# Seven products in place of eight in the input layer of two batches of a routed attention and Silu feed-forward kernel

## The chip, the cores and the metric

The kernel runs on one core of a Trainium2 chip. Its engines work side by side, each through its own list of instructions in order: TensorE (PE in the profile, with its weight loads as PEld), VectorE (DVE), ScalarE (ACT), GpSimd (POOL) and SyncE (SP), which here only issues transfers. The metric is the device time of one execution in microseconds.

## The reference

Four batches of eight heads attend over 768 tokens of 64 numbers each. Queries and keys are assigned to the nearest of 16 centroids of their head, and a query sees only keys of its own cluster. The heads' outputs are put side by side (512 numbers a token, 3072 tokens) and go through a feed-forward layer with 2048 hidden features:

```python
q_assign = np.argmax(np.einsum('bhsd,hcd->bhsc', q_n, c_n), axis=-1)
k_assign = np.argmax(np.einsum('bhsd,hcd->bhsc', k_n, c_n), axis=-1)
mask = q_assign[:, :, :, None] == k_assign[:, :, None, :]
scores = np.where(mask, scale * np.matmul(q, k.transpose(0, 1, 3, 2)), -1000000000.0)
attn = np.exp(scores - max); attn = attn / (attn.sum + 1e-09)
x = (attn @ v) laid out as (B * S, H * D)
h = x @ w_in                          # 512 -> 2048
g = h * (1.0 / (1.0 + np.exp(-h)))    # Silu
out = g @ w_out                       # 2048 -> 512
```

## The kernel before, in words

**Attention.** Queries and keys are split into a high and a low 16-bit part (`hi`, `lo`, lines 97 to 114), transposed by DMA (`ht`, line 121) into tiles of the pool "ab" (12 tiles), compared with the centroids (`l`, line 159; `ls`, `mx`, `ge` on VectorE), and the one-hot result is transposed and copied into the same tiles (`cs`, `cx`, `cv`), so that one product gives scores that are far apart where the clusters differ. A unit of attention (`qk`, line 333, and `ex`, line 338) is a pair of score products over one half of the queries (384 tokens) and one Exp over 128x768 into a tile of the pool "P" (13 tiles). Six units make two heads, which `pv` (line 350) weights with the values in 36 matmuls; `nm` divides, and `xd` (a DMA transpose on SP, line 389) or `pt` and `pe` (a transpose on TensorE and a copy) put the result, transposed, into `xts[b, c]`: batch b, half c of the tokens, four chunks of 128 numbers.

**Input layer.** For each batch, half c and block fb of 128 hidden features, `e` runs four matmuls over the four chunks (line 398) into a PSUM bank, `t` takes Tanh of half the sum into a float tile of the pool "tn" (3 tiles, line 410), and `g` (line 413, VectorE) multiplies (Tanh + 1) with the sum, which is twice the Silu, into `gt`. That is 32 units a batch, 128 in all.

**Output layer.** Pairs of token tiles (`Pair`, the `duos`) are multiplied by seven products in place of eight: `S` are sums on VectorE (line 498), `m` the products of eight matmuls (line 485), `z` copies a bank out on ScalarE (line 507), `o` combines and sends the result (lines 513 to 522), with a factor 0.5 that takes back the doubled Silu. The engine letters behind `z` and `o` in the plan have no effect.

**The order** of everything is a plan written out by hand as one list of words. A word is an operation and its number, with a letter for the engine and digits for the PSUM bank where it needs one. `step` turns each word into instructions, so each engine's order is the order of the words that concern it. Four PSUM banks are numbered 0 to 3; the other four form two double banks (tag "st") for the scores. Exp and Tanh are both read from one activation table, which is loaded once (line 567). SP's queue holds the loads, the DMA transposes and the stores in plan order; POOL's holds some loads, `cv` and casts.

Of the kernel before, what the change touches and what calls it, by code (L numbers as in the profile page):

```python
# [29 lines left out]
def kernel(  # L30
# [289 lines left out]
    NU = len(units)  # L320
    pst, Ps = {}, {}

    def qk_mm(u):
# [4 lines left out]
        qj, qn = qc[i, c]

        rhs = abs_[qj.name][:, qn : qn + 3, :].rearrange("p n c -> p (n c)")  # L330
        for e in range(2):
# [1 line left out]
            nc.tensor.matmul(pS[:, e, 0:HALF], abs_[kj.name][:, kn, :], rhs, start=True, stop=True)  # L333
# [119 lines left out]
    class Pair:  # L453

        def __init__(self, b, x, y):
            self.b, self.x, self.y = b, x, y
# [47 lines left out]

        def snap(self, n):
            o = self.half(*((0, 0), (1, 0), (1, 1))[n])
            nc.scalar.activation(out=o, in_=self.xb[:, 0:DH], func=AF.Copy, bias=0.0, scale=0.5)  # L507

        def out(self, r, c):
            t = (self.x, self.y)[r]  # L510
            o = self.half(r, c)
            if (r, c) == (0, 1):
                nc.scalar.activation(out=o, in_=self.xb[:, 0:DH], func=AF.Copy, bias=0.0, scale=0.5)
            else:
                i = self.yb[:, 0:DH] if r == 0 else self.wb[:, DH:DM]
                nc.vector.scalar_tensor_tensor(out=o, in0=i, scalar=0.5, in1=o, op0=ALU.mult, op1=ALU.add)  # L516
# [95 lines left out]
    def step(op, n, eng, banks):  # L612
# [149 lines left out]
        o11.D o10 qk86 lo24 ex86 lo22 t34 g34 qk90 ex90 pv13.1 e42.3 nm13 qk88 t42 g42 ex88 xd12 e35.0 t35 l20.2 qk93
        ex93 cx19 ge18 cs18 ht22 g35 e41.1 t41 v16.P qk91 ex91 e37.3 t37 ls20 mx20 ge20 hi23.D e39.0 qk89 t39 ex89
        qk85 g37 ex85 cx18 g39 g41 e45.2 l21.3 ls21 qk92 t45 r26 g45 e44.0 t44 g44 e46.1 lo23 mx21 ex92 ge21 qk94 ex94
        cv17 pv14.3 nm14 t46 qk100 ex100 qk95 ex95 v26.A g46 cs20 e33.2 t33 cx20 e47.0 t47 qk99 ex99 g47 pv15.3 nm15
        qk98 ex98 xd13 e43.1 t43 g33 g43 e40.0 qk97 m21.3 t40 g40 ht23 vl21.P cv20 cv19 ex97 xd14 v21.A qk101 ex101
        S23 xd15 qk109 S21 S22 l22.2 ls22 m22.1 l23.0 z20.A m26 ls23 mx23 ex109 cv18 cs21 z21.A cx21 qk108 ex108
        hi26.D qk96 r27 ex96 lo26 m25 z22.A v18.P ge23 vl25.P o20 qk107 ex107 e48.2 t48 g48 e57.0 qk110 ex110 S24
        qk106 ex106 pv16.1 nm16 t57 g57 cv21 qk103 ex103 e60.2 r25 qk104 t60 g60 e62.1 ex104 ht24 cs23 r28 qk113
        hi25.D cx23 cv23 m23 mx22 t62 g62 ex113 qk105 e53.0 ex105 ht26 lo25 qk102 ex102 l24.2 o21.A qk126 e55.1 ls24  # L770
        ge22 ex126 t53 v23.P vl27.P vl20 t55 g55 qk122 ex122 cs22 g53 cx22 r30 xd16 vl24.P pv17.2 nm17 qk111 ex111
        mx24 e49.3 t49 e52.1 qk112 xd17 ex112 t52 g49 l26.0 ls26 qk118 ex118 g52 hi27.D e63.2 t63 g63 e50.3 v20.P
        qk124 ex124 lo27 vl22 t50 cv22 qk131 ex131 e51.0 e56.1 t56 pv18.2 g50 qk117 t51 e59.3 ex117 hi28.D qk128 ex128
        g56 t59 e61.1 qk119 ex119 nm18 g51 lo28 e54.2 t54 mx26 ge26 cs26 g54 g59 qk116 ht25 ex116 r29 m27.0 qk115 S33
        o23 m31.2 ex115 t61 qk114 ex114 e58.3 qk127 xd18 hi30.P t58 ex127 g58 g61 S31 m37 qk125 ex125 qk121 S43 v27.A
        v22.P pv19.3 r31 l25.1 qk135 m24 ex121 S32 ls25 qk132 nm19 ex135 ht27 qk123 hi29.A m41.1 z30.D xd19 m36 o22
        z40.A ge24 m47 l27.3 ex132 m32.0 lo29 ht29 hi31.A cs24 z31.D o30 m35 cx24 S34 ex123 mx25 cv24 ls27 z32.A o33
        ht28 qk130 e72.0 ex130 t72 g72 qk120 ex120 e76.3 t76 mx27 lo30 qk142 m33 pv20.0 ge25 cs25 cx25 cx26 g76 ge27
        cs27 ex142 m34 o31.D o32 cx27 qk129 ex129 e73.3 v25.P qk134 S41 S42 vl30.P t73 nm20 g73 ex134 S44 pv21.2 ht30
        nm21 qk133 ex133 qk137 ex137 lo31 m46 z41.D qk139 e67.0 ex139 l29.3 ls29 qk140 qk136 t67 m45 g67 ex140 xd21  # L780
        qk143 cv26 z42.D l28.2 ex136 o43 e66.3 t66 ht31 g66 xd20 m43 pv22.0 nm22 ls28 cv25 vl28 mx28 cv27 xd22 ex143
        qk138 ex138 e69.3 t69 m44 g69 o41.D o42 e79.0 ge28 t79 qk141 qk147 ex141 ex147 e78.2 t78 vl31 g79 pv23.3 qk144
        g78 e64.1 t64 nm23 ex144 qk146 g64 e75.0 cs28 t75 mx29 ge29 g75 e77.2 cx28 e70.3 qk148 l30.1 ex146 t70 g70 t77
        g77 ex148 m42.0 ls30 mx30 qk154 ex154 e74.3 xd23 t74 g74 cs29 e68.2 ge30 t68 qk150 ex150 g68 e71.1 o40 e65.3
        t65 g65 qk145 ex145 t71 g71 cv28 e91.2 t91 cs30 e85.0 t85 g91 g85 v28.A e84.3 t84 qk155 S53 ex155 vl29.P l31.1
        g84 S51 ls31 e92.2 qk149 ex149 t92 g92 e82.0 qk151 S52 S54 m51.3 ex151 z50.D e81.1 t81 qk152 qk158 g81 t82 g82
        m56 mx31 ex158 v24.D e94.2 t94 e80.1 g94 pv24.0 m52.2 ex152 cx29 qk157 ex157 ge31 cv29 qk156 nm24 e89.0 z51.D
        o50 t80 e90.2 t90 g90 qk169 cx30 m57 cv30 t89 g89 ex169 ex156 m55 e95.2 cs31 cx31 z52.A o53 qk161 ex161 qk153
        cv31 e88.0 t95 g80 ex153 m53 g95 qk181 ex181 t88 qk162 ex162 m54 o51.A pv25.1 o52 nm25 qk160 ex160 e83.2 t83
        g83 qk165 ex165 e86.3 v29.D t86 g86 qk159 ex159 v30.D e87.1 t87 qk166 e93.2 t93 g87 g88 S63 m61.3 qk172 pv26.1  # L790
        ex166 qk167 ex172 m67 ex167 z60.D qk163 ex163 qk164 ex164 g93 v31.P S61 S62 S64 m66 z61.A qk171 ex171 m62.0
        m71.2 z70.D qk173 ex173 S73 nm26 xd26 xd25 qk180 ex180 o60 S71 m65 z62.D S72 qk176 m76 z71.D pv27.1 nm27 ex176
        qk190 ex190 m63 qk168 ex168 qk177 m75 ex177 qk170 ex170 m77 qk179 ex179 S74 z72.A o63 pv28.0 nm28 qk174 ex174
        xd24 qk178 m73 o73 qk175 m64 ex178 xd27 qk185 ex175 qk182 ex185 ex182 m72.1 o70 o62 e96.0 t96 m74 o72 g96
        o71.A qk184 ex184 o61.D e102.1 t102 qk183 ex183 pv29.0 nm29 e109.2 xd29 e106.3 qk189 ex189 qk188 pv30.0 g102
        t109 e110.1 g109 t106 ex188 g106 nm30 qk186 xd30 ex186 e103.2 t103 e97.3 t97 g103 qk191 ex191 g97 e101.0 t101
# [42 lines left out]
```

## Time and profile before

| | |
|---|---|
| time, median of 3 runs | 298.16 us (297.97 to 299.95) |
| the profiled execution's own time | 301.25 us |
| its span | 299.1 us |
| mean granted TensorE clock | 0.997 |
| TensorE busy | 288.4 us, 3433 matmuls |
| VectorE, ScalarE, GpSimd busy | 220.8, 233.9, 67.6 us |

The span runs from the first to the last instruction of the profiled execution. A group of instructions is shown as line, engine, operation, output and inputs, sizes and count, then the busy time and the mean duration of one in nanoseconds, then the idle time of the engine just before them and what ended it. In rows in order of time the columns are start, duration and what ran. Two instructions of one engine can overlap by a little, so the distance between starts is shorter than the duration of one.

### The profile page before, as it was taken

Reading aid. Unit: us, or ns where it says so; the run is one execution under the profiler, and the core shown is the slowest. Engines: PE = TensorE matmul, PEld = TensorE weight load, DVE = VectorE, ACT = ScalarE, POOL = GpSimd, SP = SyncE. Lnnn points to the kernel's source line nnn. Section 1 sums busy time; section 2 is a strip of 40 time slices with the busy share of each in tenths; the row PEclk is TensorE's granted clock in tenths of the full one; section 3 lists DMA queues with packets and bytes.
Section 4 is the critical chain, followed back from the end, with each engine's and each line's share of the span. In section 5 each row is a group of like instructions: output and inputs, shape, how many; then the busy total and the mean of one; then the engine's idle time right before and its main releaser. Section 6 shows DMA issues by size and latency. Waiting matters only on the chain.

```text
span 299.1 us, 8578 instructions
## 1 busy us (share of the span) xinstructions
PE 288.4 (96%) x3433; PEld 212.2 (71%) x3433; DVE 220.8 (74%) x484; ACT 233.9 (78%) x408; POOL 67.6 (23%) x127
## 2 busy tenths in 40 slices
PE   7899899999999999988999999999999999999994
PEld 3767666766677887666766878776777887677684
DVE  5898749689999888967779858677737533687763
ACT  5998899964989889986999977689688877854621
POOL 2656805220201124413142223222110000000000
PEclk9999999999999999999999999999999999999998
DMA  6999998999898979969978474962001103201103
GB/s 209 298 251 249 187 191 166 215 250 224 147 299 171 204 181 208 201 151 159 225 187 212 95 164 130 121 164 82 22 10 72 39 15 127 55 2 35 37 20 125
DMA packets 75208, 44.13 MB, mean 148 GB/s; under 512 B 54288, under 2 KB 70960, under 8 KB 75168
## 3 DMA queue, kind: packets, MB, share of 16 engines
q1 hardware_dynamic: 70272, 35.75, 51.1%
q0 software_dynamic: 4608, 7.54, 13.5%
q8 instruction: 27, 0.44, 0.6%
q10 hardware_dynamic: 288, 0.30, 0.3%
q14 instruction: 13, 0.11, 0.1%
HBM read 27.30 MB, written 6.29 MB: 112 GB/s over the span
## 4 chain that ended last, share of the span: by engine, by line
PE 53%; issue 2%; DMA 2%; POOL 1%; DVE 0%; POOLq 0%
PE ph L398 17%; PE xb L485 14%; PE pS L333 10%; PE pO L350 6%; PE yb L485 3%; DMA ab<-cdt 2%; PE wb L485 1%; PE psN L159 1%; POOL ab L217 0%; POOL vn L271 0%; POOL od L204 0%; DVE ot L516 0%; POOL od L205 0%; PE px L371 0%; POOLq L217 0%
## 5 line engine op out<-in xcount | busy, mean ns | idle before, releaser
L338 ACT ACTIVATE P<-pS 128x768 f16<-128x768 f32 x192 | 152.7, 816 | 20.3 <-PE pS L333 17.4
L398 PE MATMUL ph<-xt,win_s 128*128 128x384 f16 x512 | 96.8, 326 | 0.0
L333 PE MATMUL pS<-ab 128*128 128x384 f16 x384 | 87.9, 326 | 2.6 <-DMA ab<-cdt 1.3
L413 DVE SCALAR_TENSOR_TENSOR gt<-tn,ph 128x384 f16<-128x384 f32 x128 | 68.0, 549 | 26.2 <-ACT tn L410 25.4
L410 ACT ACTIVATE tn<-ph 128x384 f32<-128x384 f32 x128 | 62.1, 500 | 13.5 <-PE ph L398 12.7
L398 PEld LDWEIGHTS <-win_s 128*128 128x128 f16 x512 | 49.3, 98 | 31.0 <-DVE L L168 0.3
L333 PEld LDWEIGHTS <-ab 128*128 128x128 f16 x384 | 33.9, 98 | 17.5 <-DMA ab<-cdt 1.9
L350 PEld LDWEIGHTS <-P 128*128 128x128 f16 x1152 | 39.7, 98 | 4.5 <-issue 1.0
L350 PE MATMUL pO<-vt,P 128*128 128x65 f16 x1152 | 41.2, 193 | 0.8 <-DVE xn L362 0.8
L485 PEld LDWEIGHTS <-gt 128*128 128x128 f16 x352 | 34.0, 98 | 6.8
L112 DVE SCALAR_TENSOR_TENSOR hl<-raw,hl 128x768 f16<-128x768 f32 (+3 forms) x35 | 31.7, 908 | 0.7 <-ACT hl L103 0.5
L485 PEld LDWEIGHTS <-s 128*128 128x128 f16 x264 | 25.7, 98 | 5.5
L507 ACT ACTIVATE ot<-xb 128x256 f32<-128x256 f32 x33 | 12.7, 386 | 13.4 <-PE xb L485 13.3
L485 PE MATMUL xb<-wout_s,gt 128*128 128x256 f16 x176 | 22.6, 273 | 0.0
L159 PEld LDWEIGHTS <-ab 128*128 128x128 f16 x544 | 19.0, 97 | 3.7 <-DVE ab L146 0.4
L485 PE MATMUL xb<-wc,s 128*128 128x256 f16 x160 | 20.6, 273 | 0.0
L279 POOL CAST vt<-vn 128x384 f16<-128x384 f32 x19 | 10.8, 578 | 43.0 <-DMA vn<-in_v_dram 43.0
L159 PE MATMUL psN<-stk,ab 128*128 128x16 f16 (+1 forms) x544 | 19.9, 184 | 0.0
L105 POOL TENSOR_SCALAR hl<-raw 128x768 f16<-128x768 f32 (+1 forms) x8 | 15.8, 1979 | 14.1 <-DMA ab<-hl 8.4
L362 DVE TENSOR_TENSOR xn<-pO,zr 128x384 f16<-128x384 f32 x32 | 17.8, 557 | 1.1
L217 POOL DMA_DIRECT2D ab<-cdt x16 | 8.7, 546 | 40.7 <-PE pS L333 24.4
L204 POOL TENSOR_SCALAR od<-od 128x96 f16<-128x96 f16 x16 | 8.7, 542 | 38.6 <-DVE od L197 38.4
(93 smaller groups left out, 263.2 us busy)
## 6 DMA issues: line engine op xcount, KB each, us to landing
raw<-in_k_dram SPq DMA_DIRECT2D x31, 192.0 KB, 3.8
raw<-in_q_dram SPq DMA_DIRECT2D x24, 192.0 KB, 3.8
out_dram<-ot SPq DMA_DIRECT2D x18, 256.0 KB, 2.9
vn<-in_v_dram SPq DMA_DIRECT2D x19, 192.0 KB, 4.8
vn<-in_v_dram POOLq DMA_DIRECT2D x13, 192.0 KB, 4.1
win_s<-in_moe_w_in_dram POOLq DMA_DIRECT2D x8, 256.0 KB, 7.1
wout_s<-in_moe_w_out_dram POOLq DMA_DIRECT2D x4, 512.0 KB, 8.4
out_dram<-ot SPq DMA_DIRECT2D x12, 128.0 KB, 1.7
```

The lines of the kernel that those rows point to most:

```text
L105: nc.gpsimd.tensor_scalar(out=o, in0=i, scalar1=QS, scalar2=None, op0=ALU.mult)
L112: nc.vector.scalar_tensor_tensor(out=hl[:, s, 1, :], in0=raws[job.name][:, s, :], scalar=QS, in1=hl[:, s, 0, :], op0=ALU.mult, op1=ALU.sub ...
L159: nc.tensor.matmul(L[:, n % 2, :, n // 2], ab[:, i, :], stk[:, job.groups[i // 3][0], x : x + w], start=(x == 0), stop=(x + w == 2 * HC),)
L333: nc.tensor.matmul(pS[:, e, 0:HALF], abs_[kj.name][:, kn, :], rhs, start=True, stop=True)
L338: nc.scalar.activation(out=P, in_=pst.pop(u)[:, :, 0:HALF], func=AF.Exp, bias=0.0, scale=ESC)
L350: nc.tensor.matmul(o[:, (2 * t + h) * VW : (2 * t + h + 1) * VW], Ps[i + h, c, j // 2][:, j % 2, ts(t, 128)], vtb[(i + h) % 13][:, j, 0:VW ...
L362: nc.vector.tensor_tensor(out=xn, in0=ov[:, :, 0:D], in1=zr.unsqueeze(2).to_broadcast([128, 2 * NM, D]), op=ALU.mult)
L398: nc.tensor.matmul(ph[:, 0:HALF], win_s[:, r, ts(fb, 128)], xts[b, c][:, r, :], start=(r == 0), stop=(r == NR - 1))
L410: nc.scalar.activation(out=tn, in_=phs[b, c, fb][:, 0:HALF], func=AF.Tanh, bias=0.0, scale=0.5)
L413: nc.vector.scalar_tensor_tensor(out=gt[:, fb, NM * c : NM * c + NM, :].rearrange("p t n -> p (t n)"), in0=tns.pop((b, c, fb)), scalar=1.0 ...
L485: nc.tensor.matmul(o, self.lhs(l, f), self.rhs(r, f), start=(f == 0 and opens), stop=(f == HB - 1), skip_group_check=True)
L507: nc.scalar.activation(out=o, in_=self.xb[:, 0:DH], func=AF.Copy, bias=0.0, scale=0.5)
```

## The change

For batches 2 and 3 the input layer goes through seven products for each two-by-two block: the inner dimension is cut in two (chunks 0 and 1, chunks 2 and 3), the tokens in their two halves, and the features in fb and fb + 8. A group g (eight a batch) covers features g and g + 8 for both halves, in 7 products of 2 matmuls. Its words are:

- `ws` (16 in all, VectorE): sums of `w_in` halves, into four tiles of the pool "ab", one of the four in place; they serve both batches.
- `T` (four a batch, VectorE): differences of token halves, three into tiles of the pool "P", one in place.
- `y`: a product, by its number 1 to 7. Products 7 and 1 open two banks; 2 and 4 add onto the first, 6, 5 and 3 onto the second. A group uses two numbered banks or one double bank of the scores.
- `u` (VectorE or ScalarE): 0 copies the first bank out to a float tile of the pool "tn", 1 copies the second bank onto the first (PSUM to PSUM), 2 writes second + tile onto the first, 3 writes second + tile into the tile.
- `s` (ScalarE): Silu, from either bank or the tile, straight into `gt`.

The order within a group is thus 7, 1, u0, u1, 2, s0, 6, u2, 4, s2, 5, u3, 3, s1, s3. Tanh and `g` are gone for these two batches, and the output factor is 1.0 there. All Silu of a batch stand in one stretch of ScalarE's list, with no Exp between them.

The plan is the same up to word 619 (of 1551, now 1623). Behind that it is written anew: the attention of the later batches comes in another order, several `v` and `hi` words have another engine, the products of batch 2 stand between the words y161 and y223, those of batch 3 between y241 and y293.

```diff
+    def double(name):
+        return ps.tile([128, 2, 512], f32, name=name, tag="st", bufs=2)
...
+    def w_half(i, j, g, n):
+        return win_s[:, 2 * j : 2 * j + 2, i * DF // 2 + n * g : i * DF // 2 + n * g + n]
+
+    def w_sum(g, k):
+        if k == 0:
+            ws[g] = mp.tile([128, 3, 2, 256], f16, name="ws", tag="ab", bufs=12)
+        s2, s3, s4 = (ws[g][:, n] for n in range(3))
+        w = lambda i, j: w_half(i, j, g, 256)
+        o, a, b_, op = (
+            (s3, w(0, 0), w(1, 0), ALU.subtract),
+            (w(1, 0), w(1, 0), w(1, 1), ALU.add),
+            (s2, w(1, 0), w(0, 0), ALU.subtract),
+            (s4, w(0, 1), s2, ALU.subtract),
+        )[k]
+        nc.vector.tensor_tensor(out=o, in0=a, in1=b_, op=op)
+
+    def x_half(b, j, h):
+        return xts[b, h][:, 2 * j : 2 * j + 2, :]
+
+    def x_sum(b, k):
+        if k != 1:
+            tx[b, k] = mp.tile([128, 2, HALF], f16, name="tx", tag="P", bufs=13)
+        o, a, b_ = (
+            lambda: (tx[b, 0], x_half(b, 1, 1), x_half(b, 0, 1)),
+            lambda: (x_half(b, 0, 1), x_half(b, 0, 1), x_half(b, 0, 0)),
+            lambda: (tx[b, 2], x_half(b, 1, 1), x_half(b, 0, 1)),
+            lambda: (tx[b, 3], x_half(b, 1, 0), tx[b, 2]),
+        )[k]()
+        nc.vector.tensor_tensor(out=o, in0=a, in1=b_, op=ALU.subtract)
+
+    def group_mm(b, g, s, bk):
+        if s == 7 and bk == 4:
+            o = double("gd")
+            ys[b, g, 7], ys[b, g, 1] = o[:, 0, :], o[:, 1, :]
+        elif s in (7, 1) and (b, g, s) not in ys:
+            ys[b, g, s] = bank("gy" if s == 7 else "gx", bk)
+        o = ys[b, g, 7 if s in (7, 2, 4) else 1]
...
+        for r in range(2):
+            nc.tensor.matmul(
+                o[:, 0:HALF], w[:, r, :], x[:, r, :], start=(s in (7, 1) and r == 0), stop=(r == 1), skip_group_check=True
+            )
+
+    def group_mix(b, g, k, eng):
+        y, x = ys[b, g, 7][:, 0:HALF], ys[b, g, 1][:, 0:HALF] if k else None
+        if k == 0:
+            sbs[b, g] = mp.tile([128, HALF], f32, name="sb", tag="tn", bufs=3)
+        sb = sbs[b, g]
+        if k < 2:
+            o, i = (y, x) if k else (sb, y)
+            if eng == "D":
+                nc.vector.tensor_copy(o, i)
+            else:
+                nc.scalar.activation(out=o, in_=i, func=AF.Copy, bias=0.0, scale=1.0)
+        else:
+            nc.vector.tensor_tensor(out=(y, sb)[k - 2], in0=x, in1=sb, op=ALU.add)
+
+    def group_silu(b, g, j):
+        i = sbs[b, g] if j == 3 else ys[b, g, 1 if j == 1 else 7][:, 0:HALF]
+        f = g + NFB // 2 * (j // 2)
+        o = gt[:, f, NM * (j % 2) : NM * (j % 2) + NM, :].rearrange("p t n -> p (t n)")
+        nc.scalar.activation(out=o, in_=i, func=AF.Silu, bias=0.0, scale=1.0)
...
+            self.half_ = 0.5 if b < 2 else 1.0
...
+        gk = n // 10 // 8, n // 10 % 8
...
+        elif op == "ws":
+            w_sum(n // 4, n % 4)
+        elif op == "T":
+            x_sum(n // 10, n % 10)
+        elif op == "y":
+            group_mm(*gk, n % 10, bk)
+        elif op == "u":
+            group_mix(*gk, n % 10, eng)
+        elif op == "s":
+            group_silu(*gk, n % 10)
```

The plan around the entry into batch 2's products and out of them, and the entry into batch 3's:

```diff
+        ge28 cv25 qk149 ex149 nm23 xd22 l30.1 m46 z41.D v29.D cv27 qk145 ls30 xd23 ws3 hi31.D ex145 mx30 qk144 xd20
+        lo31 y161.0 m45 qk155 ex144 z42.A o43 ex155 cv26 l29.1 ls29 mx29 qk147 ex147 m34 qk154 ex154 ge29 ws12 qk150
+        ex150 m44 T20 qk148 ex148 o31.D ws13 ge30 T21 y167.1 u160.A u161.A y177.4 u170.D m43 ht31 cs28 T22 y171 ws5
...
+        cv29 u233 s232 u222 y224 s233 z50.A y233 y225 m61.0 u213 v30.P s212 u223 s231 s222 y213 S53 S51 S52 y223 s213
+        s223 m52.2 s211 qk156 s221 m56 ex156 qk153 ex153 z51.D pv24.3 cv31 qk151 ex151 qk181 ex181 m57 qk152 S54 m55
...
+        qk188 pv30.3 nm30 xd30 qk186 o61.D ex188 ex186 m75 pv31.1 nm31 z72.D m73 o73 pt31.0 pe31.D y241.3 T30 T31 m74
+        o72 y257.4 T32 y277.4 y247.1 y287.0 u240.D u250.A y251 o71.D u241.D u270.A y281.2 y271 y246 y242 s240 u251.D
```

More of the change, by code (lines that the diff above doesn't have):

```diff
@@ L326, in qk_mm @@
         i, c, m = units[u]
-        pS = ps.tile([128, 2, 512], f32, name="pS", tag="st", bufs=2)
+        pS = double("pS")
         qj, qn = qc[i, c]
@@ L416, in gate @@
         )
+    ws, tx, ys, sbs = {}, {}, {}, {}
+    def w_half(i, j, g, n):
[12 more added lines that the diff above has]
+        nc.vector.tensor_tensor(out=o, in0=a, in1=b_, op=op)
@@ new lines, in group_mm @@
+    def group_mm(b, g, s, bk):
[5 more added lines that the diff above has]
+        o = ys[b, g, 7 if s in (7, 2, 4) else 1]
+        h = slice(128 * (g % 2), 128 * (g % 2) + 128)
+        w = (
+            ws[g // 2][:, {7: 1, 6: 0, 3: 2}[s], :, h] if s in (7, 6, 3)
+            else w_half(*{1: (0, 0), 2: (0, 1), 4: (1, 1), 5: (1, 0)}[s], g, 128)
+        )
+        x = tx[b, {7: 0, 6: 2, 4: 3}[s]] if s in (7, 6, 4) else x_half(b, *{1: (0, 0), 2: (1, 0), 3: (1, 1), 5: (0, 1)}[s])
+        for r in range(2):
+            nc.tensor.matmul(
+                o[:, 0:HALF], w[:, r, :], x[:, r, :], start=(s in (7, 1) and r == 0), stop=(r == 1), skip_group_check=True
+            )
@@ L506, in snap @@
             o = self.half(*((0, 0), (1, 0), (1, 1))[n])
-            nc.scalar.activation(out=o, in_=self.xb[:, 0:DH], func=AF.Copy, bias=0.0, scale=0.5)
+            nc.scalar.activation(out=o, in_=self.xb[:, 0:DH], func=AF.Copy, bias=0.0, scale=self.half_)
         def out(self, r, c):
@@ L512, in out @@
             if (r, c) == (0, 1):
-                nc.scalar.activation(out=o, in_=self.xb[:, 0:DH], func=AF.Copy, bias=0.0, scale=0.5)
+                nc.scalar.activation(out=o, in_=self.xb[:, 0:DH], func=AF.Copy, bias=0.0, scale=self.half_)
             else:
                 i = self.yb[:, 0:DH] if r == 0 else self.wb[:, DH:DM]
-                nc.vector.scalar_tensor_tensor(out=o, in0=i, scalar=0.5, in1=o, op0=ALU.mult, op1=ALU.add)
+                nc.vector.scalar_tensor_tensor(out=o, in0=i, scalar=self.half_, in1=o, op0=ALU.mult, op1=ALU.add)
             self.ot[r][1] += 1
@@ L762 @@
[L762 to L796, printed above, removed]
@@ L802 @@
-        m101.1 t127 m91.2 m97 g127 m102.0 S91 z100.A S92 S94 z90.A S103 S101 m96 z91.A m107.3 m95 z92.D S102 m106 o100
-        z101.D m93 o91.A o93 m92.0 o90 m105 m94 z102.D S104 o103 o92 m103 o101.A m104 o102
+        l17.1 qk74 hi20.D lo20 od2 m4 ls17 mx17 r22 ge17 cs17 qk69 r24 cx17 ex74 qk83 m15 ls16 ex69 z12.D o13 qk82
+        ex83 pv11.1 qk80 v18.P ex82 nm11 m14 ex80 mx16 ht20 vl16.P o12 pt11.3 pe11.A qk81 ex81 qk73 ex73 l18.1 hi21.D
+        lo21 e32.3 qk78 m13 ls18 mx18 ge18 ex78 qk72 ht21 ge16 cs16 e46.1 t32 g32 o11.D l19.0 ex72 t46 ls19 qk84 cv17
@@ new lines @@
+        cx16 ex84 mx19 e35.3 t35 qk79 ex79 g35 r23 pv12.0 qk87 ex87 cs18 g46 e42.3 pv13.1 ge19 nm12 t42 g42 qk88 l20.0
+        qk86 o2 e37.3 cx18 ex88 ex86 o1.D hi22.P t37 ls20 qk93 g37 e41.0 ex93 qk90 ex90 cs19 cx19 nm13 r25 m12.2 o10
+        e36.3 lo22 ht22 hi23.D t41 g41 t36 qk85 ex85 g36 xd12 qk89 e44.1 e43.2 ex89 mx20 lo23 qk91 ex91 cv16 t44 qk94
+        ex94 hi24.P pv14.0 g44 ge20 e39.3 t39 r27 vl21.P e40.1 vl24.P nm14 ht23 xd13 g39 xd14 cv19 t40 qk92 l21.0 ls21
+        cs20 ex92 qk95 ex95 e34.3 t34 t43 qk96 ex96 pv15.0 qk98 ex98 g40 e38.1 v19.D mx21 ge21 g43 nm15 xd15 g34 t38
@@ new lines @@
+        g38 e47.2 t47 qk97 ex97 qk101 ex101 hi25.P cs21 lo24 e45.0 l22.3 ls22 g47 mx22 qk99 cv18 ex99 e33.1 t33 g33
+        t45 qk131 ex131 l23.3 qk107 lo25 ex107 g45 e56.2 t56 ls23 e58.1 g56 t58 r26 qk100 mx23 v26.P qk105 ge23 cx20
+        g58 ex105 v16.D vl20 ex100 cx21 e60.0 t60 e63.3 t63 ws8 g60 e59.2 t59 g63 S23 qk106 qk128 cv21 ex106 ge22
+        e53.1 t53 g53 pv16.0 nm16 qk104 ex128 ht24 g59 m22.3 qk103 ex104 ex103 S21 qk124 ht25 ex124 m21.1 z20.A hi27.D
+        qk112 cs23 l24.0 e55.2 S22 ls24 mx24 S24 r28 o20 qk102 ex112 ge24 t55 g55 ex102 hi26.A lo26 m26 cv20 qk109
@@ new lines @@
+        ex109 z21.A qk110 pv17.0 cs22 ex110 qk108 cx22 ex108 lo27 m25 z22.A nm17 qk126 ex126 e51.3 vl23.P cv22 qk111
+        vl22 t51 g51 r30 v20.P e50.2 l25.0 ex111 t50 g50 qk127 ex127 qk113 v21.D e49.3 v22.D ex113 t49 hi28.P lo28 m23
+        qk116 ex116 pv18.2 g49 nm18 cs24 qk115 qk130 ls25 v23.A ex115 e52.3 t52 g52 ht26 cx23 vl30.P mx25 m31.2 ex130
+        o21.A e57.0 t57 qk114 ex114 l26.3 g57 cx24 ge25 ls26 e62.1 t62 g62 cv23 qk117 ex117 e54.0 t54 g54 qk119 ex119
+        e61.3 e48.1 t61 g61 vl25.P xd16 mx26 ge26 qk118 xd18 ex118 t48 g48 m27.0 o23 vl27.P vl29.P qk138 pv19.3 ex138
@@ new lines @@
+        ht27 cv24 qk121 ex121 cs25 m24 qk125 ex125 qk123 ex123 hi30.D S33 nm19 m37 qk122 ex122 l27.1 ws9 ws10 r29 cx25
+        ht28 lo30 S43 qk120 ex120 z30.A m41.3 z40.D qk129 ex129 ls27 ht30 S31 S41 S32 xd17 pv20.1 nm20 xd19 qk142
+        ex142 qk133 ex133 m36 z31.A cs26 qk132 ex132 ws0 ws1 o22 pv21.1 mx27 ge27 cs27 qk135 l28.0 ls28 S34 S42 nm21
+        ex135 hi29.D qk136 m35 ex136 v27.D qk140 ex140 r31 cx27 lo29 qk134 ex134 m32.0 o30 qk137 ws2 m47 ws11 ex137
+        cx26 z32.D qk143 ex143 qk139 ex139 pv22.1 qk141 o33 m33 ws4 ex141 xd21 pv23.0 ht29 mx28 nm22 S44 qk146 ex146
@@ new lines @@
+        s173 ls31 y181.0 s172 y195 y201.1 u181.A y173 u200.D u201.A y182 y186 y202 u193 s192 cx28 cv28 s180 ws7 y206
+        y193 s171 u182 y237.4 y185 s200 u202 s193 s191 y184 u230.A u183 s183 y205 y217.4 v24.P u210.A u203 cx29 y231
+        y204 s182 s202 y203 y211 u231.D y236 vl28 s203 ws15 y227.2 cx30 y221.3 u211.A y232 s230 vl31 mx31 y216 u220.D
+        u221.D y212 s201 y222 y183 y226 s210 s220 ge31 cs31 cx31 u232 y234 y235 u212 y214 y215 cv30 v25.A m51.1 s181
+        cv29 u233 s232 u222 y224 s233 z50.A y233 y225 m61.0 u213 v30.P s212 u223 s231 s222 y213 S53 S51 S52 y223 s213
@@ new lines @@
+        s223 m52.2 s211 qk156 s221 m56 ex156 qk153 ex153 z51.D pv24.3 cv31 qk151 ex151 qk181 ex181 m57 qk152 S54 m55
+        ex152 qk162 ex162 o50 qk172 pv25.2 S63 v28.D ex172 z52.D o53 qk158 ex158 m67 v31.A qk164 ex164 qk171 ex171 S61
+        S73 S71 m53 S62 nm24 qk157 ex157 z60.A m54 o51.A o52 qk160 ex160 qk161 ex161 m66 qk159 ex159 z61.A m62.3 qk165
+        ex165 qk174 nm25 ex174 pv26.1 o60 nm26 S64 xd26 xd25 qk167 xd24 qk166 ex167 m71.2 qk163 ex166 qk170 ex163
+        ex170 m65 z62.D qk178 qk168 pv27.3 nm27 ex178 ex168 z70.A qk173 ex173 qk169 ex169 m72.1 qk177 ex177 qk189 m63
@@ new lines @@
+        u280.A s241 u253 s253 y261.1 y267.3 u281.D y282 y286 u273 s252 y253 s272 y273 u260.D u261.D y262 s280 u282
+        s251 y266 s273 y285 u283 y317.4 s271 s260 u262 y297.4 y284 y283 u310.D s283 y265 s282 y264 u290.A y311 y291
+        s262 u263 s263 y307.0 y301.3 u311.D s281 y312 u291.A y316 y296 y292 u300.D u301.D y302 s310 u312 y306 y315
+        s290 u292 s300 u302 y314 u313 s312 y295 y294 u293 s292 s293 y305 y263 y304 s302 S83 u303 m81.2 m87 z80.D y313
+        s313 y303 S81 S82 S84 y293 s291 s311 m86 m82.0 z81.A m85 s301 m91.3 s303 s261 S93 S91 m97 z82.A o83 S92 m84
@@ L804 @@
+        o82 z90.A m96 S103 o80 z91.A m83 m95 o81.D z92.D S94 m102.1 S101 m93 o91.D S102 S104 m101.0 z100.D o93 m92.2
+        o100 m106 z101.D o90 m94 o92 m105 z102.A m107.1 m103 o103 m104 o101.D o102
     """.split()
```

14 lines of the change are left out of this document (5 added, 9 removed).

## The prediction

> **What bounds the kernel.** I read the page first, then busy time by stretches, the waits of TensorE, the chain of waits, the groups of instructions, and at last single rows in order of time.
>
> ```profile
> PE 288.4 (96%) x3433; PEld 212.2 (71%) x3433; DVE 220.8 (74%) x484; ACT 233.9 (78%) x408; POOL 67.6 (23%) x127
> PE   7899899999999999988999999999999999999994
> PEclk9999999999999999999999999999999999999998
> ```
>
> The second line is TensorE's busy share in 40 slices: nine tenths or more from the twentieth on until the last, and the granted clock below it holds until the last. The busy time by stretches, before and behind the last idle time of TensorE:
>
> ```profile
> core 0: us, PE busy (x) PEld busy (x) DVE busy (x) ACT busy (x) POOL busy (x), PEclk, DMA share, GB/s
> 100.00:138.20 38.20, 36.08 (x452) 26.70 (x450) 31.65 (x65) 33.79 (x58) 14.22 (x28) 1.00 0.95 185
> 138.20:295.30 157.10, 157.10 (x1697) 118.49 (x1697) 105.00 (x217) 116.28 (x210) 20.42 (x41) 1.00 0.40 93
> ```
>
> From 138.2 to 295.3 us TensorE is busy in all 157.1 us, while VectorE has 105.0 and ScalarE 116.3. The plan is unchanged up to about 100 us; behind that TensorE waits just twice:
>
> ```profile
> PE pS L333 <- DMA ab<-cdt: 1.3, 1, 1.3
> PE pO L350 <- DVE xn L362: 0.8, 1, 0.8
> ```
>
> That is 2.1 us. The chain that ended last is accordingly TensorE's own order, down to its last products:
>
> ```profile
> 224.08 1.09 PE pO L350 x36
> ...
> 278.52 4.55 PE ph L398 x28
> ...
> 291.81 2.62 PE xb L485 x24
> 294.43 0.89 PE wb L485 x8
> 295.34 0.42 DVE ot L516
> ```
>
> So a matmul taken out of the last 157 us is worth its distance to the next, and whatever is added to the other engines costs nothing until TensorE waits for it. The same rows give the distances: 28 input-layer matmuls of 384 columns in 4.55 us are 0.1625 us each, so a pair of scores takes 0.325; an output product of eight matmuls takes 0.87 (24 in 2.62), the weighted sum of two heads 1.09.
>
> **What is removed.** A unit before is one block of 128 features by one half of the tokens: four matmuls (L398), one Tanh, one gate. Batches 2 and 3 have 64 units, 256 matmuls. Afterwards a group of four units takes seven products of two matmuls, 14 in place of 16, same shape: 16 groups, 224 matmuls. 32 fewer by 0.1625 is **5.2 us** off TensorE, all from the full stretch. Weight loads fall by 32 as well.
>
> **What the other engines get.** The groups of instructions:
>
> ```profile
> L338 ACT ACTIVATE P<-pS 128x768 f16<-128x768 f32 x192 | 152.7, 816 | 20.3 <-PE pS L333 17.4 <-PE pO L350 1.5
> L413 DVE SCALAR_TENSOR_TENSOR gt<-tn,ph 128x384 f16<-128x384 f32 x128 | 68.0, 549 | 26.2 <-ACT tn L410 25.4
> L410 ACT ACTIVATE tn<-ph 128x384 f32<-128x384 f32 x128 | 62.1, 500 | 13.5 <-PE ph L398 12.7
> L498 DVE TENSOR_TENSOR s<-gt 128x1024 f16<-128x1024 f16 x22 | 15.0, 687 | 0.3
> L507 ACT ACTIVATE ot<-xb 128x256 f32<-128x256 f32 x33 | 12.7, 386 | 13.4 <-PE xb L485 13.3
> L451 DVE TENSOR_TENSOR wc<-wc,wout_s 128x512 f16<-128x512 f16 x4 | 1.7, 421 | 0.1
> L567 ACT ACT_TABLE_LOAD x1 | 1.3, 1283 | 1.7 <-PEq L823 1.7
> ```
>
> VectorE loses 64 gates of 0.549 us (35.1). It gets 32 additions (two a group) and 18 of the 32 copies; they read PSUM over 384 columns as the gate does, so 50 by 0.549 is 27.5. Then 16 weight sums over 512 columns at 0.421 (6.7) and 8 token sums over 768 columns, between 0.421 and 0.687, so about 0.55 each (4.4). Net +3.5 us. ScalarE changes 64 Tanh for 64 Silu over the same 384 columns; no row shows a Silu. I price it as the Tanh. Its bounds are the 0.386 us of a 256-column copy and the 0.816 us of a 768-column Exp. It gets 14 copies at 0.5 (7.0) and table loads. The trace holds one load, 1.283 us, ahead of all Exp and Tanh. Silu alternates with Exp three times (into the stretch of batch 2, out of it, into that of batch 3); if each change is a load, that is 3.85 us. Casts moved between engines are one or two rows each way. No engine gets near 299 us in total, so only the places where the work is dense can cost.
>
> Eight of the copies per batch and eight of the additions write PSUM, which no VectorE or ScalarE row does today. Nearest rows: the gate, 0.549 us from PSUM to SBUF, and for a double pass twice that, 1.1; below, the 0.421 us of the sums that never touch PSUM. I take 0.549, since the read side is the same.
>
> **The two stretches.** Rows that stand back to back, ScalarE's first and VectorE's last, give the pace when an engine does not wait:
>
> ```profile
> 205.61 1.26 ACT L410 ACTIVATE tn<-ph 128x384 f32<-128x384 f32 x3
> 241.60 2.27 ACT L338 ACTIVATE P<-pS 128x768 f16<-128x768 f32 x3 [0.45 <-PE pS L333]
> 206.14 1.48 DVE L413 SCALAR_TENSOR_TENSOR gt<-tn,ph 128x384 f16<-128x384 f32 x3 [0.53 <-ACT tn L410]
> ```
>
> So 0.42 a Tanh, 0.76 an Exp, 0.49 a gate. In the stretch of batch 3 TensorE has 56 products of two matmuls (18.2) and seven others of 0.87 (6.1): 24.3 us. ScalarE: 32 Silu and 5 copies at 0.42, three smaller ones at 0.386, one load: 18.0. VectorE: 27 additions and copies at 0.49, four token sums at 0.55, four sums of 0.687 and one output at 0.42: 18.6. In that of batch 2 TensorE has 55 products and other work, 23.0; ScalarE 41 by 0.42, the load, and some 1.3: 19.8. TensorE stays the longest. The 39 Exp between the stretches are closest: 39 by 0.76, ten outputs of 0.386, one cast of about 0.5 and the load back make 35.3 us of ScalarE beside 36.5 us of TensorE (38 pairs of scores, 17 products, 8 weighted sums, and 0.7 of small work); 0.4 for that.
>
> Within a group the steps hang on each other: copy out (0.549), copy across (0.549), a product (0.33), Silu (0.5), addition (0.549), a product (0.33), addition (0.549), Silu (0.5): 3.9 us between taking and freeing the group's float tile. There are three such tiles, and TensorE spends 14 by 0.1625, 2.28 us, on a group; so the chain may last 6.8 us before TensorE starves, and 2.9 us are left for queueing. Walking the first groups of batch 3 through the plan with these prices I find about 5 us, with TensorE waiting now and then for a quarter of a microsecond. I put 1.4 us for the 16 groups.
>
> **The edges.** Before, the first half of the tokens entered the layer while the second was still being weighted; now the token sums need both, so the last transposes (L389, issued on SP) come straight ahead of them:
>
> ```profile
> L389 SPq DMA_TRANSPOSE xt<-xn x22: 1179/1206/2435, 92.5 to 259.4; - x22
> DMA to landing us min/median/max: 2.3/2.8/6.6
> SPq L121 <- PE pS L333: 8.1, 6, 2.1
> ```
>
> In batch 2 the plan leaves some 5 us of other TensorE work between the last of them (the word xd20) and the first product that needs a sum; the landing takes 2.8 us in the middle and 6.6 at most, so 0 to 2 us, and I take 0.6. On SP the transpose of head 29's tile (ht29) is queued just ahead of xd22, xd23 and xd20; it waits for a tile of the pool from which the weight sums now take four of twelve, and such waits last up to 2.1 us. That lies within the same 0 to 2. In batch 3 the last transpose runs through TensorE and the wait is like the 0.8 us above: 0.4. Leaving the stretch of batch 2, three sums of 0.687 follow the last additions on VectorE before the product that reads the third (m56), with some 1.9 us of TensorE work beside them: 0 to 0.8, and I take 0.4. The loads fall where ScalarE would wait for the first product, or behind the last Silu with two pairs of scores still to be worked off by TensorE: 0 here, 1.283 each if that cover is gone.
>
> **The sum.** 1.4 + 0.4 + 0.6 + 0.4 + 0.4 = 3.2 us of new waiting. The two waits of today (2.1) lie in a part whose order is rewritten; I let them go here and keep them for the range. 299.1 - 5.2 - 2.1 + 3.2 = **295.0 us of span**, 4.1 less. The profiled execution took 301.25 us, so it would take 297.1; its neighbours without the profiler have a median of 298.16, and the same 4.1 off gives **294.1**. With no new wait it is 290.9; with the 2.1 kept, and 3.2 on top, 296.2.
>
> [...] The trace has 1.283 us for its one load. [...]
>
> **The rivals.** *The switches and the dense Exp are exposed.* For: a load cannot start before the last Silu or Exp of its side, and ScalarE between the stretches has 1.2 us to spare in 36.5. Against: TensorE has work in hand at each. Three loads uncovered are 3.85 us on top of the forecast: span 298.9, **298.0**.
>
> [...]
>
> *Three float tiles are too few* (slower). If an operation that writes PSUM takes 1.1 us, copy across and the first addition grow by 0.55 each; VectorE, in order, also makes the groups behind wait, and three groups' growth falls into one group's chain, 3.3 us. 5.0 + 3.3 = 8.3 us by three tiles is 2.77 us a group against 2.28: 0.49 by 16 is 7.8 us on top of the forecast, span 302.8, **301.9**. It decides from 6.8 us between taking and freeing the tile. For: no row shows such a write, and VectorE's 18.6 us would grow by 15 times 0.55 to about 27, above TensorE's 24.3. Against: the price of every PSUM row so far goes by its columns.
>
> That the layer does not get shorter is no rival: the matmuls are counted out in the plan.
>
> **The numbers.** Forecast 0.54, exposed switches 0.26, empty engine 0.06, three tiles 0.14. About 1% (3 us) is what a measurement of this kernel can tell from no change. Faster by more means below 295.2; the forecast's own range, 290.9 to 296.2, holds that for nine tenths, and the exposed case for a fifth of its chance: 0.54. Slower means above 301.1: nearly all of the last two cases, 0.18. Within 1% is the rest, 0.28. The range from 291 to 300 leaves out the last two cases, 0.20 together.
>
> **What would show it.** Right: 3401 matmuls, TensorE's busy time down by about 5, its waits behind 100 us summing to some 3 us; Silu rows near 0.5 us; three more loads of 1.28 us. [...] If transposes land later than 5 us, the first product of batch 2 with a token sum shows it.

## The result, and the profile after

The changed kernel takes 297.64 us (median of 20 executions, 295.43 to 302.34). The kernel before, timed beside it, takes 300.03 us (20 executions). The ratio is 0.9936, with an interval of 0.9908 to 0.9964: about 1.9 us less, where 4.1 less were forecast. (The ratio leaves out the executions in the chip's slower state, so it is not the quotient of the two medians.) The forecast time of 294.1 us started from 298.16, the median of three executions; with 300.03 for the kernel before, it is the change that compares with the forecast, and not the time. Two later comparisons of the same kernel gave 0.9955 [0.9921, 0.9988] and 0.992 [0.9886, 0.9954], so the gain is there, and it is about half of the forecast. The profiled execution took 297.27 us with a span of 295.5 us. That is 3.6 us below the profiled span of before, but 1.2 us of it were already there near 99 us, where both plans are still the same (one and the same product starts at 99.79 us before and at 98.63 after), so single profiled executions cannot be compared to a microsecond.

The engines' totals and TensorE's busy share in 40 slices, from the page of the changed kernel:

```profile
PE 285.6 (97%) x3401; PEld 209.1 (71%) x3401; DVE 225.7 (76%) x498; ACT 241.4 (82%) x422; POOL 69.9 (24%) x126
PE   8899999999999999996999999999999999999995
```

The 32 matmuls are gone (3433 before, 3401 now). VectorE has 4.9 us more and ScalarE 7.5 more (3.5 and 10.85 forecast). The row of slices shows what the change did not do: the nineteenth slice, from 133 to 140 us, has a 6. Before, the dip at that place was two slices with an 8. The busy time by stretches, with the same cut as in the prediction:

```profile
core 0: us, PE busy (x) PEld busy (x) DVE busy (x) ACT busy (x) POOL busy (x), PEclk, DMA share, GB/s
100.00:138.20 38.20, 35.71 (x464) 26.28 (x463) 31.74 (x65) 32.25 (x55) 16.77 (x27) 1.00 0.92 198
138.20:292.20 154.00, 153.17 (x1642) 114.48 (x1641) 108.32 (x229) 124.07 (x226) 21.61 (x41) 1.00 0.39 92
```

Ahead of 138.2 us TensorE is idle for 2.5 us (2.1 before); behind it, 0.8 us are open where before there were none. Those 0.8 are too few: a matmul of 384 columns is shown 0.326 us long and the next can start 0.1625 us after it, so each wait loses its first 0.16 us in this view. Taken from start to start, the picture is this table. It adds up by how much the distance between two neighbouring matmuls' starts exceeds the usual distance for their shape, where that is over 15 ns, in the trace of each kernel (the later rows are the experiments below):

| us lost by TensorE | 112 to 140 us | 140 us to the end |
|---|---|---|
| before | 2.62 | 0.06 |
| changed kernel | 2.92 | 2.87 |
| the same kernel, second and third time | 1.81, 2.44 | 2.63, 2.64 |
| before without the 32 matmuls, twice | 2.92, 1.08 | 1.50, 1.51 |
| changed, without 32 more matmuls | 3.01 | 5.56 |
| changed, Tanh for Silu | 1.74 | 2.64 |
| changed, transposes early, twice | 0.05, 1.07 | 3.00, 2.59 |
| changed, three transposes early | 1.31 | 2.64 |
| changed, bank copies on VectorE | 4.33 | 6.41 |
| the last, transposes early | 2.29 | 4.84 |

The waits of TensorE behind 95 us, as the profile names them in the changed kernel:

```profile
PE ph L401 <- DMA xt<-xn: 2.4, 1, 2.4
PE ph L401 <- DVE xn L365: 0.2, 1, 0.2
```

One wait of any size, and not at a place that the prediction priced: batch 1's second half of the tokens enters the input layer (L401, the old L398), and a DMA transpose of its attention output has not landed. The chain of waits follows it back:

```profile
124.32 0.79 SPq L121
125.11 0.05 issue
125.16 6.38 DMA xt<-xn
131.54 0.03 issue
...
131.63 0.13 DVE xn L365
131.76 0.34 issue
132.11 1.01 DVE gt L416 x2
133.12 0.87 DVE hl L112
133.98 0.17 DVE L L168
134.15 4.06 DMA xt<-xn
138.21 0.04 issue
138.25 0.97 PE ph L401 x5
```

Read from below: the matmul at 138.25 us waited for a transpose that took 4.06 us to land. In front of it stand some 2.5 us of VectorE, whose `xn` buffer another transpose was still reading: that one was issued at 125.16 and landed 6.38 us later. And it was issued so late because SP was busy with the transposes of another head (L121). SP's own rows:

```profile
123.45 1.66 SPq L121 DMA_TRANSPOSE ab<-hl  x1
125.16 2.32 SPq L392 DMA_TRANSPOSE xt<-xn  x1
127.57 0.53 SPq L92 DMA_DIRECT2D raw<-in_q_dram  x1
128.15 0.43 SPq L92 DMA_DIRECT2D raw<-in_k_dram  x1
128.67 2.45 SPq L121 DMA_TRANSPOSE ab<-hl  x1
131.17 4.18 SPq L392 DMA_TRANSPOSE xt<-xn  x3
```

These are, in the plan's words, ht22, xd12, two loads, ht23, and xd13 to xd15. What the prediction had feared instead did not come. The new operations, by groups and by line:

```profile
L489 ACT ACTIVATE gt<-gd 128x384 f16<-128x384 f32 x24 | 11.5, 492 | 3.7 <-PE gd L467 1.8 <-DVE sb L483 1.8
L489 ACT ACTIVATE gt<-sb 128x384 f16<-128x384 f32 x16 | 8.3, 523 | 0.5 <-DVE sb L483 0.4
L489 ACT ACT_TABLE_LOAD x2 | 2.6, 1283 | 0.0
L341 ACT ACT_TABLE_LOAD x1 | 1.3, 1283 | 0.0
```

```profile
L483 DVE TENSOR_TENSOR gy<-gx,sb x8: 555/562/566, 197.5 to 270.7; 128x384 f32<-128x384 f32 x8
L483 DVE TENSOR_TENSOR sb<-gx,sb x8: 549/558/559, 198.8 to 272.7; 128x384 f32<-128x384 f32 x8
```

A Silu (L489) takes 492 ns out of PSUM and 523 out of SBUF, an addition (L483) 562 ns in the median when it writes PSUM and 558 when it writes SBUF, and the three new loads have 0.0 us of idle time ahead of them.

### The profile page after: what moved, and what is told of

Same layout as the page of the kernel before. It is cut to its first block, busy times and chain, and to the rows that moved or that the text cites. A ratio compares the mean times of both kernels' runs of the same rounds, so it can differ in the third digit from the quotient of the medians.

```text
span 295.5 us, 8542 instructions
## 1 busy us (share of the span) xinstructions
PE 285.6 (97%) x3401; PEld 209.1 (71%) x3401; DVE 225.7 (76%) x498; ACT 241.4 (82%) x422; POOL 69.9 (24%) x126
## 4 chain that ended last, share of the span: by engine, by line
PE 82%; DMA 7%; DVE 4%; ACT 3%; issue 1%; SPq 1%; DVEq 0%
PE pS L336 18%; PE xb L559 17%; PE ph L401 12%; PE pO L353 10%; PE gd L467 6%; PE psN L159 4%; DMA xt<-xn 4%; PE gx L467 3%; PE gy L467 3%; PE yb L559 3%; PE po L498 2%; ACT P L341 2%; DMA ab<-hl 2%; DVE hl L112 1%; DMA raw<-in_q_dram 1%
## 5 line engine op out<-in xcount | busy, mean ns | idle before, releaser
L341 ACT ACTIVATE P<-pS 128x768 f16<-128x768 f32 x192 | 150.2, 815 | 15.0 <-PE pS L336 13.3
L336 PE MATMUL pS<-ab 128*128 128x384 f16 x384 | 86.7, 326 | 0.6 <-ACT P L341 0.2
L401 PE MATMUL ph<-xt,win_s 128*128 128x384 f16 x256 | 49.3, 326 | 2.6 <-DMA xt<-xn 2.4
L416 DVE SCALAR_TENSOR_TENSOR gt<-tn,ph 128x384 f16<-128x384 f32 x64 | 34.2, 547 | 12.1 <-ACT tn L413 11.8
L336 PEld LDWEIGHTS <-ab 128*128 128x128 f16 x384 | 33.3, 98 | 13.8 <-issue 2.1
L401 PEld LDWEIGHTS <-win_s 128*128 128x128 f16 x256 | 24.6, 98 | 18.8 <-issue 3.3
L413 ACT ACTIVATE tn<-ph 128x384 f32<-128x384 f32 x64 | 31.1, 503 | 4.7 <-PE ph L401 4.2
L105 POOL TENSOR_SCALAR hl<-raw 128x768 f16<-128x768 f32 (+1 forms) x10 | 20.8, 2075 | 13.6 <-DMA ab<-hl 8.0
L159 PEld LDWEIGHTS <-ab 128*128 128x128 f16 x544 | 18.9, 97 | 4.5 <-DMA ab<-hl 0.5
L572 DVE TENSOR_TENSOR s<-gt 128x1024 f16<-128x1024 f16 x22 | 15.1, 685 | 5.3 <-PE xb L559 3.1
L279 POOL CAST vt<-vn 128x384 f16<-128x384 f32 x16 | 9.0, 572 | 39.9 <-DMA vn<-in_v_dram 39.4
```

Of the source, the lines that this page charges most:

```text
L105: nc.gpsimd.tensor_scalar(out=o, in0=i, scalar1=QS, scalar2=None, op0=ALU.mult)
L159: nc.tensor.matmul(L[:, n % 2, :, n // 2], ab[:, i, :], stk[:, job.groups[i // 3][0], x : x + w], start=(x == 0), stop=(x + w == 2 * HC),)
L341: nc.scalar.activation(out=P, in_=pst.pop(u)[:, :, 0:HALF], func=AF.Exp, bias=0.0, scale=ESC)
L401: nc.tensor.matmul(ph[:, 0:HALF], win_s[:, r, ts(fb, 128)], xts[b, c][:, r, :], start=(r == 0), stop=(r == NR - 1))
L413: nc.scalar.activation(out=tn, in_=phs[b, c, fb][:, 0:HALF], func=AF.Tanh, bias=0.0, scale=0.5)
L416: nc.vector.scalar_tensor_tensor(out=gt[:, fb, NM * c : NM * c + NM, :].rearrange("p t n -> p (t n)"), in0=tns.pop((b, c, fb)), scalar=1.0 ...
```

## The experiments

**The theory.** TensorE's distances, the operations' prices and the new waits behind 140 us are as forecast; what is missing is the 2.1 us that the prediction let go, because batch 1's transposes stand behind other heads' transposes on SP. **The rivals.** The gain itself is smaller than the matmuls' distances, since a second bound lies close behind TensorE; or the table loads cost more than they show; or ScalarE between the stretches is the bound.

**The kernel before, beside itself.**

> The kernel before, unchanged, a second time: a ratio of 1.000 within 0.3%. What it is for is the trace. If the waits around 130 to 138 us belong to the order of the plan, TensorE again loses 2 to 3 us there (2.6 in the first profile) and next to nothing behind it. If they were an accident of one execution, it loses under 1 us there.

Measured: 1.0008 [0.9967, 1.0049], 300.38 us. So the ratio's own error is some 0.4% for a run of this length. Its profiled execution was an odd one (599 us, the input layer's matmuls 0.39 us apart in place of 0.1625) and is used for nothing, so the question put to its trace is answered by others: the kernel before without 32 matmuls, below, has the same order up to 140 us, and its two traces lose 2.92 and 1.08 us there, at the places where the kernel before waited. So those waits belong to its order, but their length changes from one execution to the next.

**The removal alone.** The kernel before, with one of the four matmuls left out in every second unit of batches 2 and 3, and nothing else (it leaves out part of the sum of those features):

```diff
         for r in rs:
+            if b >= 2 and fb % 2 == 0 and r == 1:
+                continue
```

> The kernel before, in which half of the units of batches 2 and 3 leave out one of their four matmuls: 32 matmuls less (a part of the sum of those features), and nothing added or moved. My theory (TensorE is the bound from 138 us on, and a matmul taken out there is worth its distance of 0.1625 us): 5.2 us less, ratio 0.983. Rival (in executions without the profiler something else is the bound for part of that stretch, so that the removal itself is worth only what the change brought): 1.5 to 2.5 us less, ratio 0.992 to 0.995.

Measured: 295.82 us, 0.988 [0.9837, 0.9923], about 3.6 us less. A second time:

> The kernel before with the 32 matmuls left out and nothing else (outputs of batches 2 and 3 are then not the reference's), once more. Theory (a matmul taken out of the full stretch is worth its distance): 5.2 us, 0.983. Rival (the stretch has a second bound close behind TensorE, so part of it turns into waiting): 3 to 4 us, 0.987 to 0.990.

Measured: 296.3 us, 0.9874 [0.9835, 0.9913], about 3.8 us. The forecast distance of 5.2 us would be 0.983, just outside both intervals. The table says where the rest went: 1.5 us of small waits behind 140 us, in both traces and at the same places, the longest 0.29 us. 5.2 - 1.44 is 3.8 (0.06 of the 1.5 were there before). So the full stretch was only just full, and other engines' hand-offs end right behind TensorE's. Which of them bounds each place was not followed further. Ahead of 140 us the waits that the profile names are, in the first trace and in the second:

```profile
PE pS L333 <- DMA ab<-cdt: 2.6, 2, 2.2
```

```profile
PE pO L350 <- DVE xn L362: 0.9, 1, 0.9
```

They are the two places that the prediction showed for the kernel before.

**Removal on top of the change.** In two of a group's seven products (numbers 2 and 5) one of the two matmuls is left out:

```diff
-        for r in range(2):
+        for r in range(1, 2) if s in (2, 5) else range(2):
```

> The changed kernel, in which products 2 and 5 of every group leave out one of their two matmuls: 32 matmuls less (half of the inner dimension of these two products). My theory (small hand-offs aside, TensorE is still the bound in the stretches): a further 4 to 5.2 us, so a ratio to the kernel before of about 0.977 to 0.981. Rival (ScalarE, VectorE and the chain within a group have become the bound there): under 2.5 us further, a ratio above 0.985.

Measured: 295.63 us, 0.9871 [0.9817, 0.9924]. Against the 0.9936 of the changed kernel that is about 2 us for another 32 matmuls worth 5.2, though the two ratios were not timed side by side. The table shows 2.7 us of further waits behind 140 us. Beside the transpose, the profile names two waits inside a group: TensorE waiting for VectorE's copy across and for its addition:

```profile
PE ph L401 <- DMA xt<-xn: 2.8, 1, 2.8
PE gy L467 <- DVE gy L479: 0.3, 1, 0.3
PE gx L467 <- DVE gy L483: 0.2, 1, 0.2
```

The rival is right to this extent: the rewritten kernel has hardly any slack left in its groups.

**Batch 1's transposes early.** In SP's order xd12 and xd13 move up, each right behind what makes its data:

```diff
-  qk86 o2 e37.3 cx18 ex88 ex86 ... cs19 cx19 nm13 r25 m12.2 o10
-  e36.3 lo22 ht22 ... g36 xd12 qk89 ... nm14 ht23 xd13 g39 xd14
+  qk86 o2 e37.3 cx18 xd12 ex88 ex86 ... cs19 cx19 nm13 xd13 r25 m12.2 o10
+  e36.3 lo22 ht22 ... g36 qk89 ... nm14 ht23 g39 xd14
```

> The changed kernel, in which the DMA transposes xd12 and xd13 stand in SP's order right behind the results that they move, and no longer behind the transpose ht22 and, for xd13, a load of raw queries and ht23. My theory (the wait of 2.5 us at batch 1's second half is the queueing of these four transposes on SP): the wait falls under 0.7 us and the time by 2 to 2.5 us against the changed kernel, a ratio to the kernel before of 0.985 to 0.987. Rival (the transfers themselves are the bound up to 140 us, and the wait only moves): the same time as the changed kernel, 0.992 to 0.995, with the wait elsewhere between 120 and 145 us.

Measured: 296.56 us, 0.9882 [0.9848, 0.9915], a little above the 0.985 to 0.987 expected, and the wait is gone from the trace (0.05 us between 112 and 140 us). Then beside the changed kernel on one chip:

> The changed kernel once more, as the reference for the next two. Both theories: 0.994 to 0.996 of the kernel before. In its trace, TensorE idle between 112 and 140 us by 1.8 to 3.0 us, waiting for a DMA transpose of batch 1.

> The changed kernel with batch 1's transposes xd12 and xd13 moved forward in SP's order, each right behind the step that makes its data, now beside the changed kernel on the same chip. Theory (the wait for them is where the missing part of the gain lies): 0.987 to 0.990, that is 1.5 to 2 us below the changed kernel. Rival (the first run differed by its chip): within 0.5 us of the changed kernel, 0.993 to 0.997.

> As the run before, and xd14 ahead of ht23 as well. Theory that any transpose queued behind a head's transposes can still be late in some executions: 0.984 to 0.988, a further 0.3 to 1 us, with no wait at all for batch 1's second half. Rival (what is left is no wait for transposes, or ht23 is now late for its own reader): the same as the run before, or up to 0.5 us above it.

Measured: the changed kernel 297.8 us, 0.992 [0.9886, 0.9954]; with two transposes early 296.13 us, 0.986 [0.9817, 0.9904]; with xd14 ahead of ht23 too, 295.46 us, 0.9857 [0.9813, 0.99]. From the single times on that chip, the means differ by 1.8 us [0.8, 2.9] and 2.0 us [1.0, 2.9]. So the 1.5 to 2 us expected of two early transposes came; the changed kernel's own 0.992 is below the 0.994 to 0.996 expected of it, though its interval reaches there. In the second trace with two transposes early a part of the wait is left, which the first such trace did not have:

```profile
PE ph L401 <- DMA xt<-xn: 0.7, 1, 0.7
```

The chain leads it back to the last of the half's four transposes (xd15, issued at 134.10 us and landed 3.25 us later), which was not moved. The third early transpose is worth nothing that these runs can tell. In its trace no matmul of the input layer waits for a transpose any more; what is left there is a wait for a head's own queries and keys:

```profile
PE psN L159 <- DMA ab<-hl: 1.1, 1, 1.1
```

That is the case which the rival had named: ht23, now behind xd14, comes late for its own reader. SP's rows of this trace, which are xd12, xd13, ht22, xd14, ht23 and xd15:

```profile
119.40 1.24 SPq L392 DMA_TRANSPOSE xt<-xn  x1
...
122.64 1.22 SPq L392 DMA_TRANSPOSE xt<-xn  x1
...
125.56 2.17 SPq L121 DMA_TRANSPOSE ab<-hl  x1
...
129.95 1.19 SPq L392 DMA_TRANSPOSE xt<-xn  x1
131.23 1.30 SPq L121 DMA_TRANSPOSE ab<-hl  x1
132.62 1.74 SPq L392 DMA_TRANSPOSE xt<-xn  x1
```

The first transpose of the half (xd12) goes out at 119.40 us in place of 125.16. From issue to landing, the 22 transposes (L392) of the changed kernel and those of this one take:

```profile
DMA to landing us min/median/max: 2.3/2.6/6.4
```

```profile
DMA to landing us min/median/max: 2.3/2.4/5.1
```

This version, with three transposes early, is faster than both kernels.

**The table loads.** Tanh in place of Silu, so that the three loads go (the values of batches 2 and 3 are then other ones), beside the changed kernel:

```diff
-        nc.scalar.activation(out=o, in_=i, func=AF.Silu, bias=0.0, scale=1.0)
+        nc.scalar.activation(out=o, in_=i, func=AF.Tanh, bias=0.0, scale=1.0)
```

> The changed kernel, unchanged, beside the next three on one chip: the ratio that was found, 0.9936, within 0.4%. In the trace TensorE loses 2.5 to 3 us between 112 and 140 us again if that wait belongs to the plan, and 2.5 to 3 us in all behind 186 us.

> The changed kernel with Tanh in place of every Silu (so another function of the hidden features): no table loads behind the first, the same instructions otherwise. My theory (all three loads are covered by work that TensorE has in hand): the time of the changed kernel within 0.4%. Rival (the switches are exposed): 1.3 us less for each load that is, up to 3.85 us, and TensorE waits gone behind 196, 215 and 257 us.

Measured: 0.9955 [0.9921, 0.9988] with the loads, 0.9963 [0.9926, 0.9999] without. The loads cost nothing that shows, in the times (to about a microsecond) or in the table (2.63 and 2.64 us lost behind 140 us). ScalarE's rows around the first of the three in the changed kernel show no gap at it either:

```profile
195.18 0.49 ACT L481 ACTIVATE sb<-gd 128x384 f32<-128x384 f32 x1
195.68 1.28 ACT L489 ACT_TABLE_LOAD   x1
196.98 0.49 ACT L489 ACTIVATE gt<-gy 128x384 f16<-128x384 f32 x1
```

The load starts 0.01 us behind the end of the last copy, and the first Silu 0.02 us behind the load.

**ScalarE between the stretches.** The bank copies of batch 2's output (the words z50 to z72) go from ScalarE to VectorE; and the same with xd12 and xd13 early:

```diff
-            nc.scalar.activation(out=o, in_=self.xb[:, 0:DH], func=AF.Copy, bias=0.0, scale=self.half_)
+            if self.b == 2:
+                nc.vector.tensor_scalar(out=o, in0=self.xb[:, 0:DH], scalar1=self.half_, scalar2=None, op0=ALU.mult)
```

> The changed kernel, in which the nine bank copies of batch 2's output products (the words z50 to z72) run on VectorE in place of ScalarE: 3.4 us less for ScalarE where the Exp are dense. My theory (the TensorE waits between the two stretches, 1.45 us, come from ScalarE being full there): these waits fall below 0.6 us, the time by 0.8 to 1.3 us against the changed kernel. Rival (they are the grain of the order, two score banks that come free in turn): the waits stay at 1.2 us or more, the time the same.

> The early transposes and the bank copies on VectorE together. If both waits were real and independent: 2.5 and 1.0 us less than the changed kernel, a ratio to the kernel before of 0.980 to 0.984, and TensorE idle behind 112 us under 2.5 us in all. If one of the two waits only moves: 0.986 to 0.989.

Measured: 300.0 us, 1.004 [1.0004, 1.0077], and with the transposes early 298.23 us, 0.9972 [0.9934, 1.001]. Relieving ScalarE in this way makes the kernel slower by 0.85% against 0.9955 on the same chip. The four gaps of 0.22 to 0.29 us between score products stay at their length (at 236, 241, 246 and 250 us), so those copies on ScalarE do not make them. What is new is a 1.4 us wait near 256 us, where a product needs the bank that VectorE now copies. (Of the 6.41 us in the table, another 1.6 are matmuls at the halved clock of the last section.) Together, the two edits did not reach either of the ratios expected. The early transposes are again worth 2.1 us [0.8, 3.3] between the two, although waits of 2.2 us together are still in the second's trace, the longer one again for xd15: this comparison bears the theory out in time and not in its one trace.

## Why the prediction was right or wrong

- **Removal: "32 fewer by 0.1625 is 5.2 us off TensorE".** The count is right (3401 matmuls), and so is the distance. "So a matmul taken out of the last 157 us is worth its distance to the next" is not: alone it brought 3.6 and 3.8 us. The 157.1 us without idle time were read as a reserve in the other engines; they only say that nobody was later than TensorE, not by how much. In the sum for this change the error would not appear twice, if what this bound takes is part of the new waits below; no run separates the two.
- **New waits: 3.2 us.** Measured behind 140 us: 2.87, 2.63 and 2.64 us against 0.06 before. The sum is right within 0.6, its parts less so: errors in both directions made up for each other, and that was luck. Hand-offs within the stretches: 1.4 forecast, 0.82 found (0.25 in batch 2, the rest in batch 3). Between the stretches: 0.4 forecast, 0.99 found, in four gaps. Entry into batch 2: 0.6 forecast, nothing found. Exit from it at m56: 0.4 forecast, 0.21 found. Entry into batch 3: 0.4 forecast, 0.37 found. Another 0.24 lies at 189 us in this one trace of the three, at a step that the prediction did not speak of, and the rest are gaps of about 0.1 and less.
- **"The two waits of today (2.1) lie in a part whose order is rewritten; I let them go".** This is the step that failed. TensorE lost 2.92, 1.81 and 2.44 us between 112 and 140 us, against 2.62 in the profile of before (2.92 and 1.08 in the two further traces of that order): the two named waits are gone, and one for a transpose stands in their place. Behind 100 us the waits sum to 5.8, 4.4 and 5.1 us, where some 3 were forecast. With 2.1 kept the prediction's own text has 296.2 us, 2.0 less than the 298.16 it started from, which is about what was measured. The experiment that takes this wait away brings 1.8 us [0.8, 2.9] and with it the gain that was forecast. The cause was visible in the row quoted for the edge into batch 2, a landing of up to 6.6 us, and in the plan: xd12 to xd15 behind ht22 and ht23. The kernel before has it the other way round, xd12 ahead of ht22 and xd13 ahead of ht23, so the rewriting itself made the wait. Its SP rows (L389 is `xd`, L121 is `ht`):

```profile
122.30 1.19 SPq L389 DMA_TRANSPOSE xt<-xn  x1
...
124.89 1.45 SPq L121 DMA_TRANSPOSE ab<-hl  x1
...
131.72 1.25 SPq L389 DMA_TRANSPOSE xt<-xn  x1
133.08 1.44 SPq L121 DMA_TRANSPOSE ab<-hl  x1
134.62 3.05 SPq L389 DMA_TRANSPOSE xt<-xn  x2
```

The prediction asked how late the transposes land for batch 2, where other work covers it, and not for batch 1's second half.
- **VectorE and ScalarE prices.** Additions and copies to PSUM were priced at 0.549 us and took 0.554 to 0.567 on VectorE. The Silu was priced as a Tanh at 0.5 and took 0.49 to 0.52. ScalarE's copies at 0.5 took 0.48 to 0.50. The rival of too few float tiles (301.9 us) hung on a 1.1 us write and falls with it. The additions, which read PSUM, took 558 ns in the median to SBUF and 562 to PSUM.
- **Exposed switches (298.0 us).** The time, 297.64, only looks close to this rival's: as a change the rival says 0.2 us less, and 1.9 were measured. Its mechanism did not come either: three loads of 1.283 us are there, none is waited for by TensorE, and the kernel without them is no faster (0.9963 against 0.9955). **An empty engine (0.06 of the chances)** was an assumption of the author's, and no run shows it: the three loads have 0.0 us of idle time ahead of them in the groups, start 0.01 to 0.02 us behind the end of the operation before them, and cost nothing that the time shows.
- **The account.** 5.2 less for the matmuls, 2.65 more behind 140 us (the mean of three traces, 2.71, less 0.06), and 2.39 in place of 2.21 ahead of it (means of three traces each: 2.92, 1.81 and 2.44 against 2.62, 2.92 and 1.08) make 2.4 less. Measured were 1.9, 1.3 and 2.4 less. The difference is within the intervals, about 0.9 us each way, and what it consists of stays open.
